# A gated-linear-attention and gated-SSM kernel: whole-row loads of w_in, the transfers of the first two xT on GpSimd's queue, and the second group's attention ahead of the first projection

## The chip, the core and the metric

The kernel runs on one core of one Trainium2 chip. The time is device microseconds of that core, from launch to end. The kernel before was timed 9 times, and one further execution was recorded by the hardware profiler.

## The reference

Two blocks follow one another. The first is a gated linear attention over 4 batches, 8 heads, 768 steps and head width 48; the second projects its output, runs a decaying sum along the sequence, gates it and projects it back.

```python
for t in range(S):                       # attention, per batch and head
    state = alpha[t, :, None] * state + k[t][:, None] * v[t][None, :]
    y[t] = q[t] @ state
x = y.transpose(0, 2, 1, 3).reshape(B, S, H * D)          # 4 x 768 x 384
proj = x @ w_in                                           # 384 x 1024
val, gate = proj[..., :512], proj[..., 512:]
for t in range(S):
    h = exp(A_log) * h + val[:, t]
    ys[:, t] = h
out = (gate * sigmoid(gate) * ys) @ w_out                 # 512 x 384
```

The two weight matrices arrive as float64. The kernel reads them as pairs of 32-bit words and makes float32 of them.

## The kernel before, in words

The sequence of each batch is cut into three groups of 256 steps, so there are 12 groups, and each group has two chunks (c = 0, 1) of 128 steps. The function `fast` does all the work; `general` is a second version that runs only if a flag that `fast` computes says that the inputs were out of its range. `fast` is scheduled by hand: every engine executes its instructions in the order in which the code issues them, and the framework adds only the waits. SP, ScalarE (ACT) and, in principle, GpSimd (POOL) can issue DMAs; each DMA reports its end through one of a few shared completion counters, and a DMA that is given a counter waits until the DMA that had it earlier has landed.

**Loads.** Groups 0 to 2 load alpha, k and q in natural layout (`pair`, `load_natural`, L411 to L421: one DMA of 196.6 KB for each chunk). Groups 3 and up load them in another layout (`loads`, `load_raw`, L396). `load_v` brings v. `load_w` (L442) brings w_in in three units of columns (128, 128 and 256 of each half), eight DMAs each, and w_out in two; the rows of w_in are reordered on the way, so that a 128-partition tile holds rows for partitions 0 to 47, 48 to 63, 64 to 111 and 112 to 127.

**Weights to float32.** `convert` (L506) makes one unit: ScalarE copies the low words (L518), VectorE (DVE) does two operations on the high words (L519, L521), and GpSimd adds both (L523). `check_w` (L525) takes the largest and smallest magnitude of each unit, late in the kernel.

**Attention of a group m.** `natural_alpha` (L558) transposes alpha on TensorE (PE), ScalarE copies it (L564). `products` (L593) makes running products of alpha with two scans on VectorE (`prod` L606 and, backwards, `inv` L618). `natural_qk` (L566) transposes k and q, and its `times` (L580) multiplies them by the products into Z. `scores` (L645) multiplies Z's k and q halves into PSUM, `masks` (L655) puts the masked result in A: half on ScalarE and GpSimd (L658, L659), half on VectorE (L660). `keys` (L636) transposes Z's keys, ScalarE copies them (L643). `state` (L686) accumulates the running state in PSUM and ScalarE copies it (S_sb, L695). `values` (L662) multiplies A by v into y, `carried` (L674) adds the part of earlier chunks. `join` (L697) copies y to xT, one half on ScalarE (L701) and one on VectorE (L702), and issues six DMAs of 16 KB that move rows of xT to other partitions (L705).

**Second block of a group n.** For each of four column blocks cc, `project` (L711) does six matmuls into pv and pg (L720), and `gated` (L724) does a scan on VectorE (hh, L727), a Silu on ScalarE (sg, L732) and a product on GpSimd (f, L733). `output` (L735) does the second projection (L741), copies and stores it. I call the work of the loop over n (L821) for one n a turn.

**Order.** Ahead of the loop stand the attention of group 0, part of that of group 1, and `convert(0)`. Turn n holds the second block of group n and, between its four projections, the attention of group n + 1 and the preparation (`products`) of group n + 2. Turn 0 also holds the rest of the conversions of w_in (`convert(1)`, `convert(2)`, `convert(2, 1)`, L850 to L872) and both of w_out (L893, L895), and turns 0 and 1 do Z's multiplications in their middle (L848, L853). In turns 0 and 1 and ahead of the loop, all six DMAs of `join` are issued by ScalarE; from turn 2 on, three by SP and three by ScalarE (L886).

## Time and profile before

| | us |
|---|---|
| median of 9 runs (lowest to highest) | 339.62 (338.27 to 342.66) |
| the profiled execution's own time | 341.38 |
| its span, first to last instruction | 339.6 |
| busy: PE, DVE, POOL, ACT | 296.4, 232.4, 105.6, 91.6 |
| mean granted TensorE clock | 0.949 |

A time in the trace counts from the start of the span. A row of a timeline gives start, duration (both us), engine, line, operation, what it writes and reads, how many were merged, and in brackets the idle time of the engine ahead of it with what ended it. An engine with a q behind it (SPq, ACTq) is its sequencer, here issuing a DMA. Lines are those of the kernel before. A busy engine may be waiting inside an instruction, so busy time alone does not show which engine sets the pace.

### The profile page before, as it was taken

Reading aid. Unit: us, or ns where it says so; the run is one execution under the profiler, and the core shown is the slowest. Engines: PE = TensorE matmul, PEld = TensorE weight load, DVE = VectorE, ACT = ScalarE, POOL = GpSimd, SP = SyncE. Lnnn points to the kernel's source line nnn. Section 1 sums busy time; section 2 is a strip of 40 time slices with the busy share of each in tenths; the row PEclk is TensorE's granted clock in tenths of the full one; section 3 lists DMA queues with packets and bytes.
Section 4 is the critical chain, followed back from the end, with each engine's and each line's share of the span. In section 5 each row is a group of like instructions: output and inputs, shape, how many; then the busy total and the mean of one; then the engine's idle time right before and its main releaser. Section 6 shows DMA issues by size and latency. Waiting matters only on the chain.

```text
span 339.6 us, 5950 instructions
## 1 busy us (share of the span) xinstructions
PE 296.4 (87%) x2341; PEld 234.4 (69%) x2341; DVE 232.4 (68%) x256; ACT 91.6 (27%) x188; POOL 105.6 (31%) x97
## 2 busy tenths in 40 slices
PE   3983869149997995999999999999999999999992
PEld 3672748127874882886887877878878788787771
DVE  3855772461994794499799899998988969633110
ACT  4161321311411411322412415124133152131111
POOL 6022272140431420080351601804416036041020
PEclk9998789878998999699999999999999999999997
DMA  9994996833208908960873937909749230100101
GB/s 135 177 175 95 174 271 127 209 46 95 67 0 188 241 12 164 245 99 12 221 144 104 225 52 188 179 12 242 123 121 223 38 93 3 58 1 14 47 5 53
DMA packets 68269, 39.71 MB, mean 117 GB/s; under 512 B 47364, under 2 KB 66952, under 8 KB 68232
## 3 DMA queue, kind: packets, MB, share of 16 engines
q1 hardware_dynamic: 65744, 38.30, 55.9%
q10 hardware_dynamic: 2488, 0.94, 1.3%
q8 instruction: 20, 0.33, 0.5%
q14 instruction: 17, 0.14, 0.1%
HBM read 33.33 MB, written 4.72 MB: 112 GB/s over the span
## 4 chain that ended last, share of the span: by engine, by line
PE 64%; DMA 12%; DVE 9%; SPq 5%; issue 4%; POOL 1%; ACTq 1%; ACT 1%; DVEq 0%; POOLq 0%
PE pv L720 17%; PE o L741 16%; PE pg L720 15%; PE sc L652 5%; DMA wbits<-in_moe_w_in_dram 5%; PE y L671 5%; DMA raw_q<-in_q_dram 3%; PE y L682 2%; PE st L692 2%; DMA raw_k<-in_k_dram 2%; SPq L420 2%; PE tp L642 2%; DVE prod L606 2%; DMA v<-in_v_dram 1%; DVE Z L597 1%
## 5 line engine op out<-in xcount | busy, mean ns | idle before, releaser
L733 POOL TENSOR_TENSOR f<-sg,hh 128x256 f32<-128x256 f32 x48 | 57.8, 1205 | 173.1 <-ACT sg L732 162.2
L720 PE MATMUL pv<-xT,w_in 128*128 128x256 f32 x288 | 77.4, 408 | 14.1 <-POOL w_in L523 9.9
L741 PE MATMUL o<-w_out,f 128*128 128x384 f32 x192 | 68.4, 510 | 14.0 <-POOL w_out L523 11.5
L720 PEld LDWEIGHTS pv<-xT,w_in 128*128 128x128 f32 x288 | 55.6, 200 | 28.1 <-POOL w_in L523 10.8
L720 PE MATMUL pg<-xT,w_in 128*128 128x256 f32 x288 | 73.2, 392 | 0.0
L741 PEld LDWEIGHTS o<-w_out,f 128*128 128x128 f32 x192 | 37.6, 197 | 39.5 <-POOL w_out L523 12.9
L720 PEld LDWEIGHTS pg<-xT,w_in 128*128 128x128 f32 x288 | 57.1, 198 | 8.6
L732 ACT ACTIVATE sg<-pg 128x256 f32<-128x256 f32 x48 | 18.4, 384 | 133.6 <-PE pg L720 77.3
L727 DVE TENSOR_TENSOR_SCAN hh<-a_dec,hh,pv 128x256 f32<-128x256 f32 x32 | 23.5, 735 | 41.4 <-PE pv L720 39.5
L659 POOL TENSOR_TENSOR A<-A,mask 128x512 f32<-128x512 f32 x24 | 31.9, 1351 | 30.1 <-ACT A L658 30.1
L606 DVE TENSOR_TENSOR_SCAN prod<-aT,first 128x1024 f32<-128x1024 f32 x12 | 32.8, 2730 | 0.1
L618 DVE TENSOR_TENSOR_SCAN inv<-aT,last 128x1025 f32<-128x1025 f32 x12 | 31.0, 2585 | 0.4
L671 PE MATMUL y<-A,v 128*64 128x128 f32 x384 | 23.9, 274 | 1.6 <-POOL A L659 1.6
L652 PE MATMUL sc<-Z 48*128 48x128 f32 x384 | 25.1, 278 | 0.1
L652 PEld LDWEIGHTS sc<-Z 48*128 48x128 f32 x384 | 22.7, 188 | 2.8 <-issue 2.1
L745 ACT ACTIVATE o_sb<-o 128x384 f32<-128x384 f32 x24 | 11.8, 490 | 47.6 <-PE o L741 47.6
L727 DVE TENSOR_TENSOR_SCAN hh<-a_dec,pv 128x256 f32<-128x256 f32 x16 | 10.9, 680 | 19.2 <-PE pv L720 19.0
L671 PEld LDWEIGHTS y<-A,v 128*64 128x64 f32 x384 | 20.7, 137 | 2.2 <-POOL A L659 2.1
L660 DVE TENSOR_TENSOR A<-sc,mask 128x512 f32<-128x512 f32 x24 | 16.4, 689 | 7.2 <-PE sc L652 6.9
L597 DVE STREAM_TRANSPOSE aT<-raw_a 128x1024 f32<-128x1024 f32 x9 | 18.4, 2040 | 0.0
L597 DVE STREAM_TRANSPOSE Z<-raw_q 128x1024 f32<-128x1024 f32 x9 | 18.3, 2035 | 0.0
L597 DVE STREAM_TRANSPOSE Z<-raw_k 128x1024 f32<-128x1024 f32 x9 | 18.2, 2020 | 0.0
(82 smaller groups left out, 251.2 us busy)
## 6 DMA issues: line engine op xcount, KB each, us to landing
raw_k<-in_k_dram SPq DMA_DIRECT2D x24, 192.0 KB, 5.0
raw_q<-in_q_dram SPq DMA_DIRECT2D x24, 192.0 KB, 5.3
v<-in_v_dram SPq DMA_DIRECT2D x24, 192.0 KB, 4.4
out_dram<-o_sb SPq DMA_DIRECT2D x24, 192.0 KB, 1.9
raw_a<-in_alpha_dram SPq DMA_DIRECT2D x23, 192.0 KB, 3.9
raw_a<-in_alpha_dram SPq DMA_DIRECT2D x18, 176.0 KB, 3.9
raw_k<-in_k_dram SPq DMA_DIRECT2D x18, 176.0 KB, 5.1
raw_q<-in_q_dram SPq DMA_DIRECT2D x18, 176.0 KB, 4.1
```

Of the source, the lines that this page charges most:

```text
L597: nc.vector.transpose(out=to.rearrange("p h (c j) -> p h j c", j=NT), in_=raw_bufs[m % NR][name].rearrange("p h (j d) -> p h j d", d=D)[:, ...
L606: nc.vector.tensor_tensor_scan(out=prod, data0=aT[:, 0:4 * GC], data1=first.rearrange("p h n -> p (h n)"), initial=0.0, op0=ALU.mult, op1= ...
L618: nc.vector.tensor_tensor_scan(out=inv[:, ::-1], data0=aT[:, ::-1], data1=last.rearrange("p h n -> p (h n)")[:, 0:4 * GC + 1][:, ::-1], in ...
L652: nc.tensor.matmul(sc[i][:, p, :], Z[rows, p, 1, cols], Z[rows, p, 0, cols], start=True, stop=True)
L659: nc.gpsimd.tensor_mul(A[:, 1], A[:, 1], mb)
L660: nc.vector.tensor_mul(A[:, 0], sc[0], mb)
L671: nc.tensor.matmul(ys[m][i][ds(64 * s, 64), e, ds(c * C, C)], v_sb[:, c, 2 * p + i, :], A[:, i, p, :], start=(c == 0 and e == 0), stop=Fal ...
L720: nc.tensor.matmul(pj, w_in[:, kk, vg, ds(cc * C, C)], xT[:, kk, :], start=(kk == 0), stop=(kk == NK - 1))
L727: nc.vector.tensor_tensor_scan(out=hh, data0=a_dec[:, cc:cc + 1].to_broadcast([C, GC]), data1=pv, initial=prev_h[cc][:, GC - 1:GC] if g el ...
L732: nc.scalar.activation(sg, pg, AF.Silu)
L733: nc.gpsimd.tensor_mul(fs[n][:, cc, :], sg, hh)
L741: nc.tensor.matmul(os[c], fs[n][:, cc, ds(c * C, C)], w_out[:, cc, :], start=(cc == 0), stop=(cc == NI - 1))
```

## The change

- w_in is loaded in whole rows (8 KB): four DMAs in place of 24, the first two (partitions 0 to 63) on SP, the other two (64 to 127) on ScalarE's queue after `masks` of group 0. k and q of group 1 are issued ahead of all weights, w_out right after v of group 1, and alpha, k and q of group 2 after that.
- The attention of group 1 is finished ahead of the loop, and with it all four conversions of w_in. Four more warming matmuls stand in PE's order ahead of it. `masks` of group 0 goes ahead of `keys`.
- Turn 0 has no attention any more. The two conversions of w_out follow the second and the third projection, and alpha of group 2 is transposed after the second. Z of group 2 is finished at the end of turn 0, not in the middle of turn 1. Turn 1 has the order of the later turns.
- In `join`, ScalarE copies both halves of y, in every group. The six DMAs of groups 0 and 1 are issued by GpSimd, those of group 2 by SP and ScalarE as in later groups.
- The buffer for the low words has two copies in place of one, and `check_w` takes the rows of w_in in three units.

SyncE's queue (SP), the start, from the loads of v of group 0 on. In the names, raw_k_83, raw_q_82 and v_85 belong to group 1, raw_a_78, raw_k_80 and raw_q_79 to group 2 here, wbits and bits to the weights. Before:

```order
L429 DMA v_84<-in_v_dram 128x8x48 x2
L450 DMA wbits_88<-in_moe_w_in_dram 48x3x256 x4
L450 DMA wbits_88<-in_moe_w_in_dram 16x3x256 x4
L420 DMA raw_k_83<-in_k_dram 128x8x48 x2
L420 DMA raw_q_82<-in_q_dram 128x8x48 x2
L450 DMA wbits_89<-in_moe_w_in_dram 48x3x256 x4
L450 DMA wbits_89<-in_moe_w_in_dram 16x3x256 x4
L429 DMA v_85<-in_v_dram 128x8x48 x2
L450 DMA wbits_90<-in_moe_w_in_dram 48x3x512 x4
L450 DMA wbits_90<-in_moe_w_in_dram 16x3x512 x4
L420 DMA raw_a_78<-in_alpha_dram 128x8x48 x2
```

And now:

```order
L429 DMA v_84<-in_v_dram 128x8x48 x2
L420 DMA raw_k_83<-in_k_dram 128x8x48 x2
L420 DMA raw_q_82<-in_q_dram 128x8x48 x2
L443 DMA bits_in<-in_moe_w_in_dram 48x3x2048
L443 DMA bits_in<-in_moe_w_in_dram 16x3x2048
L429 DMA v_85<-in_v_dram 128x8x48 x2
L448 DMA bits_out<-in_moe_w_out_dram 128x2x768 x2
L420 DMA raw_a_78<-in_alpha_dram 128x8x48 x2
L420 DMA raw_k_80<-in_k_dram 128x8x48 x2
L420 DMA raw_q_79<-in_q_dram 128x8x48 x2
```

The k and q of group 1 stand ahead of all weights, and the 24 issues of w_in have become two here (the other two are on ScalarE's queue).

GpSimd (POOL), from `masks` of group 0 on. A_254, A_265 and A_444, A_455 are the masks of groups 0 and 1 before; A_229, A_240 and A_376, A_387 now. f is the gated product. Before:

```order
L659 TENSOR_TENSOR A_254<-A_254,mask_97 128x512
L659 TENSOR_TENSOR A_265<-A_265,mask_97 128x512
L523 TENSOR_TENSOR w_in_86<-w_in_86,wr_356 128x6x128
L733 TENSOR_TENSOR f_399<-sg_410,hh_408 128x256
L523 TENSOR_TENSOR w_in_86<-w_in_86,wr_417 128x6x128
L659 TENSOR_TENSOR A_444<-A_444,mask_97 128x512
L659 TENSOR_TENSOR A_455<-A_455,mask_97 128x512
L523 TENSOR_TENSOR w_in_86<-w_in_86,wr_462 128x6x128
L733 TENSOR_TENSOR f_399<-sg_477,hh_475 128x256
L523 TENSOR_TENSOR w_in_86<-w_in_86,wr_480 128x6x128
```

And now, with xT_324 and xT_480 the xT of groups 0 and 1:

```order
L652 TENSOR_TENSOR A_229<-A_229,mask_94 128x512
L652 TENSOR_TENSOR A_240<-A_240,mask_94 128x512
L698 DMA xT_324<-xT_324 16x256 x6
L652 TENSOR_TENSOR A_376<-A_376,mask_94 128x512
L652 TENSOR_TENSOR A_387<-A_387,mask_94 128x512
L515 TENSOR_TENSOR w_in_86<-w_in_86,wr_406 128x6x128
L515 TENSOR_TENSOR w_in_86<-w_in_86,wr_411 128x6x128
L515 TENSOR_TENSOR w_in_86<-w_in_86,wr_416 128x6x128
L515 TENSOR_TENSOR w_in_86<-w_in_86,wr_421 128x6x128
L698 DMA xT_480<-xT_480 16x256 x6
L726 TENSOR_TENSOR f_503<-sg_514,hh_512 128x256
L726 TENSOR_TENSOR f_503<-sg_527,hh_525 128x256
```

Six DMAs stand ahead of the masks of group 1, the four additions for w_in stand together behind these masks, and six more DMAs stand ahead of the first product f.

TensorE (PE), from the transposes of group 1's q to the attention of group 1. Before:

```order
L574 MATMUL tn_372<-ident_96,raw_q1_82 128x128 x4
L574 MATMUL tn_377<-ident_96,raw_q1_82 128x128 x4
L720 MATMUL pv_400<-xT_347,w_in_86 128x256 x3
L720 MATMUL pg_401<-xT_347,w_in_86 128x256 x3
L642 MATMUL tp_422<-ident_96,Z_361 128x128 x4
L642 MATMUL tp_428<-ident_96,Z_361 128x128 x4
```

And now, the attention of group 1 from its keys on, in the same place:

```order
L635 MATMUL tp_388<-ident_93,Z_333 128x128 x4
L635 MATMUL tp_394<-ident_93,Z_333 128x128 x4
L685 MATMUL st_110<-v1_85,ktm0_97 64x48 x8
L664 MATMUL y0_436<-A_376,v1_85 64x128 x4
L664 MATMUL y1_437<-A_376,v1_85 64x128 x4
L664 MATMUL y0_436<-A_387,v1_85 64x128 x4
L664 MATMUL y1_437<-A_387,v1_85 64x128 x4
L685 MATMUL st_110<-v1_85,ktm1_98 64x48 x8
```

Sixteen matmuls of `carried` follow; their end and the first projections stand so:

```order
L675 MATMUL y0_436<-Z_333,S_sb_434 48x128
L675 MATMUL y1_437<-Z_333,S_sb_434 48x128
L713 MATMUL pv_504<-xT_324,w_in_86 128x256 x3
L713 MATMUL pg_505<-xT_324,w_in_86 128x256 x3
L713 MATMUL pv_517<-xT_324,w_in_86 128x256 x3
L713 MATMUL pg_518<-xT_324,w_in_86 128x256 x3
L556 MATMUL tn_530<-ident_93,raw_a0_78 128x128 x4
L556 MATMUL tn_536<-ident_93,raw_a0_78 128x128 x4
```

The first projection (pv) followed the transposes of q directly before; now the scores, keys, states and values of group 1 are ahead of it.

The diff, cut to its core:

```diff
+    bits_in = const.tile([C, NK, 2 * DI, 2], U32, name="bits_in")
+    bits_out = const.tile([C, NI, DM, 2], U32, name="bits_out")
+
+    def load_w_in(half, engine):
+        for row, size, first, step in ((64 * half, D, 4 * half * D, D), (64 * half + D, R, (4 * half + 3) * D, R)):
+            engine.dma_start(out=bits_in[ds(row, size)].rearrange("p kk n two -> p kk (n two)"),
+                             in_=moe_w_in.bitcast(U32)[ds(first, NK * step)]
+                             .rearrange("(kk p) n -> p kk n", p=step)[0:size])
...
-        r = p1.tile([C, x, y, z], I32, tag="wr", name="wr")
+        r = p2.tile([C, x, y, z], I32, tag="wr", name="wr")
...
         nc.scalar.activation(xT[:, 1::2], y[1], AF.Copy)
-        nc.vector.tensor_copy(out=xT[:, 0::2], in_=y[0])
+        nc.scalar.activation(xT[:, 0::2], y[0], AF.Copy)
...
     load_v(0, SP)
-    load_w(0, SP)
     pair("k", 1, SP, SP)
     pair("q", 1, SP, SP)
-    load_w(1, SP)
+    load_w_in(0, SP)
     load_v(1, SP)
+    for i in range(2):
+        load_w_out(i, SP)
...
+    def warm(count):
+        t = ps_mm.tile([C, 4, C], FP32, tag="mm", name="warm")
+        for _ in range(count):
+            nc.tensor.matmul(t, ident, ident[:, None, :].to_broadcast([C, 4, C]), start=True, stop=True)
+    warm(5)
...
     for c in range(G):
+        masks(0, c)
+    load_w_in(1, ACT)
+    for c in range(G):
         keys(0, c)
-    for c in range(G):
-        masks(0, c)
...
-    join(0, (ACT, ACT))
-    convert(0)()
+    join(0, (nc.gpsimd, nc.gpsimd))
     k_times, q_times = natural_qk(1, "k"), natural_qk(1, "q")
+    warm(4)
     for _ in steps:
         pass
+    for c in range(G):
+        k_times(c)
+        q_times(c)
+    for c in range(G):
+        scores(1, c)
+    for c in range(G):
+        keys(1, c)
+    for c in range(G):
+        masks(1, c)
+    for i in range(NI):
+        convert(i)()
+    state(1, 0)
+    values(1, 0)
+    values(1, 1)
+    state(1, 1)
+    carried(1, 0)
+    carried(1, 1)
+    join(1, (nc.gpsimd, nc.gpsimd))
...
-        att = m < N
+        att = 0 < n < N - 1
...
         gated(n, 1, *pj)
+        if nat:
+            natural_alpha(n + 2)
+            check_alpha(n + 2)
+            convert(NI)()
+        else:
             go(1)
         pj = project(n, 2)
         gated(n, 2, *pj)
+        if nat:
+            convert(NI + 1)()
+        else:
             go(2)
...
-            join(m, (ACT, ACT) if n < 2 else (SP, ACT))
+            join(m, (SP, ACT))
...
         if nat:
             k_times, q_times = natural_qk(n + 2, "k"), natural_qk(n + 2, "q")
+            for c in range(G):
+                k_times(c)
+                q_times(c)
```

More of the change, by code (lines that the diff above doesn't have):

```diff
@@ L781, in fast @@
     k_times, q_times = natural_qk(0, "k"), natural_qk(0, "q")
-    load_w(2, SP)
-    pair("a", 2, SP, SP)
-    for i in range(3, NW):
-        load_w(i, SP)
-    pair("k", 2, SP, SP)
-    pair("q", 2, SP, SP)
-    warm = ps_mm.tile([C, 4, C], FP32, tag="mm", name="warm")
-    for _ in range(5):
-        nc.tensor.matmul(warm, ident, ident[:, None, :].to_broadcast([C, 4, C]), start=True, stop=True)
+    for name in "akq":
+        pair(name, 2, SP, SP)
+    def warm(count):
[3 more added lines that the diff above has]
+    warm(5)
     for _ in products(0):
@@ L845, in fast @@
         gated(n, 0, *pj)
[L846 to L855 removed]
+        if att:
             attend()
@@ L858, in fast @@
             go(1)
-        if n == 1:
-            pj = project(n, 1)
-            gated(n, 1, *pj)
-            attend()
         if att:
@@ L876, in fast @@
         gated(n, 2, *pj)
-        if not nat:
+        if nat:
+            convert(NI + 1)()
+        else:
             go(2)
```

78 lines of the change are left out of this document (19 added, 59 removed).

## The prediction

> **What bounds the kernel now.** I read the page first, then busy time by stage (the windows), then TensorE's timeline with what ended its idle time, then the waits of the SP queue.
>
> ```profile
> span 339.6 us, 5950 instructions
> GB/s 135 177 175 95 174 271 127 209 46 95 67 0 188 241 12 164 245 99 12 221 144 104 225 52 188 179 12 242 123 121 223 38 93 3 58 1 14 47 5 53
> ```
>
> The windows below are cut at the first projection of each turn. The columns are the stretch, its length, busy time of PE, PEld, DVE, ACT and POOL, the granted clock, the DMA share and GB/s.
>
> ```profile
> 32.97:82.54 49.57, 33.80 (x224) 25.35 (x225) 23.79 (x27) 12.30 (x22) 15.02 (x11) 0.80 0.76 151
> 82.54:108.33 25.79, 22.85 (x182) 17.58 (x181) 21.48 (x22) 5.87 (x12) 7.76 (x6) 0.98 0.36 89
> 108.33:135.93 27.60, 23.40 (x186) 18.54 (x184) 18.92 (x18) 7.44 (x16) 6.88 (x6) 0.93 0.70 144
> 135.93:161.36 25.43, 25.43 (x201) 20.39 (x202) 19.68 (x20) 6.46 (x14) 8.96 (x6) 0.90 0.58 118
> 161.36:183.10 21.74, 21.74 (x182) 17.41 (x181) 19.74 (x21) 6.13 (x13) 8.80 (x6) 1.00 0.63 146
> 183.10:205.80 22.70, 22.70 (x188) 18.40 (x188) 20.49 (x20) 7.44 (x16) 6.90 (x6) 1.00 0.66 140
> 205.80:228.54 22.74, 22.28 (x199) 17.91 (x198) 21.76 (x22) 6.57 (x14) 8.85 (x6) 1.00 0.64 140
> 228.54:339.60 111.06, 104.14 (x811) 82.93 (x809) 66.75 (x80) 28.26 (x61) 32.94 (x28) 0.98 0.34 78
> ```
>
> From turn 4 on (161.36), PE is busy without a gap at full clock: a turn takes 21.74 to 22.74 us, and only less work for PE could shorten it. Turn 0 takes 49.57 us with 33.80 busy at clock 0.80, and turns 1 to 3 take 25.4 to 27.6. So the first 161 us hold the idle time. These rows say what PE waited for.
>
> ```profile
> 32.97 2.93 PE L720 MATMUL pv<-xT,w_in 128*128 128x256 f32 x6 [5.65 <-POOL w_in L523]
> 35.69 2.77 PE L720 MATMUL pg<-xT,w_in 128*128 128x256 f32 x6
> ...
> 48.69 2.64 PE L720 MATMUL pv<-xT,w_in 128*128 128x256 f32 x6 [2.95 <-POOL w_in L523]
> ...
> 69.59 2.93 PE L741 MATMUL o<-w_out,f 128*128 128x384 f32 x4 [8.86 <-POOL w_out L523]
> ...
> 106.31 2.23 PE L741 MATMUL o<-w_out,f 128*128 128x384 f32 x4 [2.50 <-POOL f L733]
> ...
> 135.93 0.76 PE L720 MATMUL pv<-xT,w_in 128*128 128x256 f32 x1 [4.20 <-issue]
> ```
>
> Up to 70 us PE waits for converted weights; at 106 and 136 for f and, as no engine is named, I take it, for an xT that lands late. Behind both stand SP's waits and one of its issues:
>
> ```profile
> SPq L405 <- DMA xT<-xT: 33.0, 12, 15.2
> ...
> SPq L450 <- DMA xT<-xT: 5.4, 1, 5.4
> ```
>
> ```profile
> 86.97 17.04 SPq L405 DMA_DIRECT2D raw_k<-in_k_dram  x4
> ```
>
> Loads of k and w_in share no data with xT, yet SP stood until xT transfers had landed, once for 15.2 us: four issues of raw_k took 17.04 us.
>
> **The change, part by part.** I follow the new order to the first projection (T0), then add turns.
>
> *Start to Z of group 1.* Up to group 0's scores only loads move. The rows of before that matter:
>
> ```profile
> 11.08 4.65 PE L791 MATMUL warm<-ident 128*128 128x512 f32 x10
> ...
> 26.23 1.09 PE L574 MATMUL tn<-ident,raw_q 128*128 128x128 f32 x8 [0.25 <-DVE xT L702]
> ```
>
> ```profile
> 25.51 0.66 DVE L702 COPY xT<-y 128x512 f32<-128x512 f32 x1
> 26.09 0.55 DVE L519 TENSOR_SCALAR w_in<-wbits 128x768 uint32<-128x768 uint32 x1
> 26.67 0.96 DVE L521 SCALAR_TENSOR_TENSOR w_in<-wbits,w_in 128x768 uint32<-128x768 uint32 x1
> ...
> 27.96 2.29 DVE L618 TENSOR_TENSOR_SCAN inv<-aT,last 128x1025 f32<-128x1025 f32 x1
> ...
> 36.54 0.67 DVE L580 TENSOR_TENSOR Z<-tn,inv 128x512 f32<-128x512 f32 x1
> ```
>
> The copy and the two converting operations (0.66 + 0.55 + 0.96 = 2.2 us) leave DVE's path ahead of inv, which ends at about 28.1 in place of 30.25. Four products for Z (0.6 apart) end at 30.5. On PE, q of group 1 ends at 27.3, and four warming matmuls follow: five took 4.65, so four take 3.7, to 31.0. They cover the wait for Z and cost at most 0.5 us.
>
> *Attention of group 1.*
>
> ```profile
> 39.48 2.06 PE L652 MATMUL sc<-Z 48*128 48x128 f32 x32
> ```
>
> ```profile
> 39.58 1.08 ACT L643 ACTIVATE ktm<-tp 128x512 f32<-128x512 f32 x2
> ```
>
> Scores take 31.0 to 33.0, keys to 34.0; DVE's two masks end at 33.7; on ACT two ktm and two copies of A (about 1.1 each pair) take 33.5 to 35.9, so GpSimd's first mask can start at 35.3.
>
> *The four conversions.* GpSimd's add and DVE's operations collide, and the trace shows how:
>
> ```profile
> 46.83 1.80 POOL L523 TENSOR_TENSOR w_in<-w_in,wr 128x768 int32<-128x768 int32 x1 [1.56 <-DVE w_in L521]
> ```
>
> ```profile
> 47.20 1.85 DVE L519 TENSOR_SCALAR w_in<-wbits 128x768 uint32<-128x768 uint32 x1
> ```
>
> ```profile
> 20.60 2.50 POOL L659 TENSOR_TENSOR A<-A,mask 128x512 f32<-128x512 f32 x2 [14.66 <-ACT A L658]
> ```
>
> L519 takes 0.55 us alone; started at 47.20 inside the add, it ended at 49.05, 0.42 after the add. So I let the two take turns. From 33.7 DVE does unit 0 and half of unit 1 (0.55 + 0.96 + 0.55 = 2.06, to 35.8); then in turn two masks (1.25 each), two adds (1.80 each) and, between them, 0.96 + 0.55 + 0.96 on DVE: the second add ends at 44.4. Without collisions it would be at 35.3 + 2.5 + 3.6 = 41.4.
>
> ACT now matters, for its copy of the fourth unit's low words waits for the second add's buffer, and S_sb, which the rest of the attention needs, stands behind it in ACT's order.
>
> ```profile
> 38.77 0.92 ACT L518 ACTIVATE wr<-wbits 128x768 int32<-128x768 uint32 x1
> ```
>
> ```profile
> 23.07 0.33 ACT L695 ACTIVATE S_sb<-st 128x192 f32<-128x192 f32 x1
> ```
>
> ```profile
> 53.16 0.67 PE L692 MATMUL st<-v,ktm 128*64 128x48 f32 x16
> ...
> 55.97 1.09 PE L682 MATMUL y<-Z,S_sb 48*48 48x128 f32 x32
> ```
>
> 44.4 + 0.92 + 0.33 + 0.67 + 1.09 gives T0 = 47.4, rounded to 47; without collisions 44.4. The third add ends at about 46.7 and the fourth at 49.5, ahead of their projections.
>
> *Whole rows.* For this w_in must have landed by 33.7. By then 14 loads of 196.6 KB (2.75 MB) and w_in (3.15 MB) must come, with v and w_out beside its end. The second slice of the GB/s row (177) and the sixth (271, mostly longer rows) bound the rate; a slice is 8.49 us. The first two slices (135 and 177) carry 2.65 MB, so the 14 loads are through at about 18; ACT issues its half of w_in after its two copies of A, at about 19. Counted from 20, 3.15 MB take 11.6 us at 271 (to 31.6) or 17.8 at 177 (to 37.8). I take the upper rate, as the rows get longer, not shorter; the lower one costs 4 us.
>
> *Turn 0.* PE idles about 5 us ahead of T0, so it starts slow, as at 32.97, where pv and pg took 2.93 and 2.77. Warm matmuls of a projection, transposes and the output are these:
>
> ```profile
> 84.00 1.29 PE pg L720 x6
> ```
>
> ```profile
> 80.80 1.04 PE L574 MATMUL tn<-ident,raw_k 128*128 128x128 f32 x8
> ...
> 126.40 5.32 PE L741 MATMUL o<-w_out,f 128*128 128x384 f32 x16
> ```
>
> Eight times 1.29 is 10.3, three sets of transposes 2.6 (two fill 80.80 to the first pv at 82.54), output 5.3, slow start 2.7 (about twice 2.85 less 1.46): 20.9 us, to 67.9. The scans for group 2 (2 x 2.29) and both w_out conversions fall beside it.
>
> *xT on GpSimd.* The trace has no DMA issued there. The nearest rows:
>
> ```profile
> 25.04 0.60 ACT L701 ACTIVATE xT<-y 128x512 f32<-128x512 f32 x1 [0.30 <-PE y L682]
> ...
> 57.88 4.00 ACTq L705 DMA_DIRECT2D xT<-xT  x6
> ```
>
> Six issues took ACT 4.00, or 0.67 each; as an upper bound I take 0.67 + 2.29 = 3.0, one scan of DVE ahead of each. For the first join, GpSimd has from 26.2 to 35.3, so 1.5 each is free. For the second, it starts at 49.5, and two f, an add and a third f (4.0 us) must follow before output at 61.2 needs them: 1.3 each is free. I take 1.0, near the ACT row: cost nothing. At 3.0 it costs 9 + 10 = 19 us. This takes 4 us of issuing off ACT in each early join.
>
> *Copies on ACT.* The second copy costs ACT 0.60 a turn and frees 0.67 of DVE. A copy on DVE may stand behind a scan, one on ACT need not; xT comes sooner or at worst 0.6 later, which projection 3 and the output cover (2.6 + 5.3). Nothing.
>
> *Turns 1 to 3.* With all of attention 1 and Z of group 2 done earlier, turn 1 has the form of the turn at 161.36, turn 2 of that at 183.10, turn 3 of that at 205.80: 21.74 + 22.70 + 22.74 = 67.2, against 25.79 + 27.60 + 25.43 = 78.8 now.
>
> *The rest.* 21.74 + 22.70 + 22.74 + 111.06 = 178.2, unchanged; `check_w` reads as many words as before.
>
> Sum: 47 + 20.9 + 67.2 + 178.2 = 313.3, against a span of 339.6, so 26.3 less. The profiled execution took 341.38, 0.5% above the median 339.62. I put the difference at the median: 339.62 - 26.3 = 313.3, say 313. About 0.5% is what a measurement of this kernel can tell from no change.
>
> **The rivals.**
>
> *Turns 1 to 3 keep their waits.* If SP still stands behind transfers of xT, the 11.6 us stay: 325. For it: 33.0 us of such waits. Against: GpSimd's DMAs need not share SP's counters. Chance 0.17.
>
> *Weights late.* w_in at 177 GB/s, 4 us, with v and w_out in between up to 8: 317 to 321. Against: slice six. Chance 0.1.
>
> *GpSimd is slow at issuing.* At 2 us each, the first six cost 3.0 and the second 4.2: 320. At 3.0, 332. For it: the collisions above; against: ahead of the first projection DVE does only some 6 us in the time of each join. [...] Chance 0.1.
>
> *Slower.* The same place, with a larger price: the twelve issues stand between GpSimd's masks, adds and f, which PE needs. Free are 9 + 8 = 17 us; to use up 26.3 they must take 43 together, 3.6 each, and beyond 3.7 the kernel is slower by 0.5%; at 4.0 it is 344. Against: this is six times the ACT row. Chance 0.03.
>
> *No whole-row gain and waits as before* together (w_in 8, turns 11.6, GpSimd 7): 339, no change. Chance 0.03.
>
> **How the numbers follow.** The forecast has 0.57. Its own range is 308 (no collisions, no slow start) to 318. Up to the first rival, the range reaches 326 and leaves out GpSimd's worse prices and some of what is below. Faster by over 0.5%: all but the last two, 0.94, less 0.01 for what I did not think of: 0.93; same 0.03; slower 0.04.
>
> **What would show it.** Right: the first pv at 44 to 49 with w_in landed by 34; no gap of PE over 1 us in turns 1 to 3, at 67 us for the three; SP's waits for xT short; GpSimd's issues near 1 us. Wrong: a first pv past 52, PE waiting for f in turn 0, turns of over 24 us, or weights that land after 37.

## The result, and the profile after

The changed kernel takes 325.15 us (median of 10 runs, 322.64 to 326.76) where the kernel before took 340.43 beside it: a ratio of 0.9551, with a 95% interval of 0.9519 to 0.9582. Ratios here leave out executions more than 1.5% above the fastest of the same kernel; the medians include them. The gain is 15 us where 26 were forecast. The profiled execution has a span of 325.4 against the sum's 313.3, so the miss to explain is 12.1 us.

The page's first line and its row of bytes moved (40 slices of 8.14 us; the line numbers of this section and of the experiments are those of each run's own kernel):

```profile
span 325.4 us, 5980 instructions
GB/s 134 163 155 161 126 256 176 227 73 49 233 98 87 238 75 141 221 28 170 207 44 241 112 86 237 74 150 218 23 197 182 63 48 11 52 1 14 48 5 55
```

The windows, cut as before at the first projection of each turn (length, busy time of PE, PEld, DVE, ACT and POOL, granted clock, DMA share, GB/s):

```profile
0.00:55.24 55.24, 32.99 (x323) 25.27 (x324) 31.13 (x41) 17.05 (x30) 19.27 (x32) 0.86 1.15 166
55.24:80.89 25.65, 22.77 (x92) 17.12 (x89) 14.06 (x16) 7.36 (x14) 13.97 (x13) 0.84 0.63 119
80.89:102.62 21.73, 21.73 (x183) 17.39 (x182) 19.38 (x20) 6.10 (x13) 8.81 (x6) 1.00 0.67 136
102.62:124.79 22.17, 22.17 (x186) 17.95 (x184) 18.29 (x17) 7.45 (x17) 6.91 (x6) 1.00 0.69 143
124.79:147.40 22.61, 22.61 (x202) 18.39 (x200) 19.04 (x19) 7.45 (x17) 8.98 (x6) 1.00 0.66 140
147.40:325.40 178.00, 170.80 (x1375) 136.83 (x1373) 125.22 (x133) 51.72 (x112) 57.74 (x46) 0.99 0.46 102
```

Set against the sum, row by row: T0 is 55.24 for 47 (8.2 too late), turn 0 is 25.65 for 20.9 (4.75 too long), turns 1 to 3 are 66.5 for 67.2, the rest 178.0 for 178.2. Both misses lie ahead of 81 us, and PE has no gap in turns 1 to 3. The timeline around T0, with the idle time before each row and what ended it:

```profile
18.94 24.53 SPq L448 DMA_DIRECT2D bits_out<-in_moe_w_out_dram  x2
...
44.79 0.56 DVE L511 TENSOR_SCALAR w_in<-bits_in 128x768 uint32<-128x768 uint32 x1 [12.47 <-DMA bits_in<-in_moe_w_in_dram]
45.13 1.09 PE L685 MATMUL st<-v,ktm 128*64 128x48 f32 x16 [10.86 <-DMA v<-in_v_dram]
...
51.47 0.93 ACT L510 ACTIVATE wr<-bits_in 128x768 int32<-128x768 uint32 x1 [2.03 <-POOL w_in L515]
...
52.67 0.76 PE L685 MATMUL st<-v,ktm 128*64 128x48 f32 x16 [3.00 <-ACT S_sb L688]
...
55.24 2.93 PE L713 MATMUL pv<-xT,w_in 128*128 128x256 f32 x6
```

DVE had stood for 12.47 us when w_in came, at 44.8 in place of the 31.6 that the sum used; v, queued behind w_in, came as late. The two halves of w_in, on two queues, did not move side by side. ScalarE issued its half at 18.22, but from 20 to 24 us SP's queue (q1) alone moves, and from 36 to 40 ScalarE's (q10) moves most of the bytes, at 125 and 120 GB/s:

```profile
18.22 0.82 ACTq L443 DMA_DIRECT2D bits_in<-in_moe_w_in_dram  x2
```

```profile
q1 hardware_dynamic: 61, 0.50, 97.8%
```

```profile
q10 hardware_dynamic: 78, 0.48, 94.0%
```

The columns of the last two are packets, MB and the share of the 16 DMA engines' time. From w_in's landing on, the chain is the one forecast: adds and DVE take turns (L513, 0.96 us ahead of the first add, takes 2.44 to 2.46 beside the first three), ACT's copy waits for the second add, S_sb for ACT. Then, in turn 0:

```profile
69.19 2.64 DVE L599 TENSOR_TENSOR_SCAN prod<-aT,first 128x1024 f32<-128x1024 f32 x1
69.65 3.78 POOL L515 TENSOR_TENSOR w_out<-w_out,wr 128x768 int32<-128x768 int32 x1
...
73.48 5.83 PE L734 MATMUL o<-w_out,f 128*128 128x384 f32 x12 [2.87 <-POOL w_out L515]
```

The second addition for w_out starts inside DVE's scan and takes 3.78 us where one in the first projections' chain took 1.81 to 2.00; PE waits for it 2.87 us, and then runs the twelve matmuls slowly, at a granted clock of 0.84 in this turn and of 0.52 from 73.48 to 76.40. e4 comes back to both. SP's loads of a, k and q no longer wait for transfers of xT (33.0 us before); the row is gone from the waits of SP's queue.

### The profile page after: what moved, and what is told of

It reads as the page before. It is cut to its first block, busy times and chain, and to the rows that moved or that the text cites. A ratio compares the mean times of both kernels' runs of the same rounds, so it can differ in the third digit from the quotient of the medians.

```text
span 325.4 us, 5980 instructions
## 1 busy us (share of the span) xinstructions
PE 293.1 (90%) x2349; PEld 233.0 (72%) x2349; DVE 227.1 (70%) x244; ACT 97.1 (30%) x200; POOL 115.7 (36%) x109
## 4 chain that ended last, share of the span: by engine, by line
PE 80%; DMA 9%; DVE 3%; POOL 3%; ACT 2%; issue 0%; ACTq 0%; DVEq 0%; POOLq 0%
PE pv L713 21%; PE o L734 19%; PE pg L713 19%; DMA bits_in<-in_moe_w_in_dram 8%; PE sc L645 7%; PE y L664 5%; PE y L675 3%; PE st L685 3%; PE tp L635 2%; DMA a_log<-in_moe_A_log_dram 1%; POOL w_in L515 1%; POOL w_out L515 1%; ACT wr L510 1%; DVE inv L611 1%; DVE prod L599 1%; DVE Z L573 1%
## 5 line engine op out<-in xcount | busy, mean ns | idle before, releaser
L726 POOL TENSOR_TENSOR f<-sg,hh 128x256 f32<-128x256 f32 x48 | 60.6, 1262 | 144.7 <-ACT sg L725 143.5
L713 PE MATMUL pv<-xT,w_in 128*128 128x256 f32 x288 | 73.5, 392 | 0.0
L713 PE MATMUL pg<-xT,w_in 128*128 128x256 f32 x288 | 71.0, 383 | 0.0
L734 PE MATMUL o<-w_out,f 128*128 128x384 f32 x192 | 66.0, 498 | 2.9 <-POOL w_out L515 2.9
L713 PEld LDWEIGHTS pv<-xT,w_in 128*128 128x128 f32 x288 | 53.6, 193 | 12.1 <-issue 2.2
L720 DVE TENSOR_TENSOR_SCAN hh<-a_dec,hh,pv 128x256 f32<-128x256 f32 x32 | 23.5, 733 | 33.5 <-PE pv L713 31.6
L652 POOL TENSOR_TENSOR A<-A,mask 128x512 f32<-128x512 f32 x24 | 30.0, 1271 | 35.6 <-ACT A L651 35.6
L611 DVE TENSOR_TENSOR_SCAN inv<-aT,last 128x1025 f32<-128x1025 f32 x12 | 29.4, 2449 | 0.4
L685 PE MATMUL st<-v,ktm 128*64 128x48 f32 x320 | 13.5, 229 | 13.9 <-DMA v<-in_v_dram 10.9
L685 PEld LDWEIGHTS st<-v,ktm 128*64 128x64 f32 x320 | 11.8, 142 | 17.8 <-issue 14.0
L664 PEld LDWEIGHTS y<-A,v 128*64 128x64 f32 x384 | 22.4, 145 | 0.2 <-issue 0.2
```

The costliest lines, as they stand in the source:

```text
L611: nc.vector.tensor_tensor_scan(out=inv[:, ::-1], data0=aT[:, ::-1], data1=last.rearrange("p h n -> p (h n)")[:, 0:4 * GC + 1][:, ::-1], in ...
L652: nc.gpsimd.tensor_mul(A[:, 1], A[:, 1], mb)
L664: nc.tensor.matmul(ys[m][i][ds(64 * s, 64), e, ds(c * C, C)], v_sb[:, c, 2 * p + i, :], A[:, i, p, :], start=(c == 0 and e == 0), stop=Fal ...
L685: nc.tensor.matmul(st[ds(64 * i, 64), p, :], ktms[c][:, p, i, :], vs[m % NV][:, c, 2 * p + i, 0:D], start=(ch == 0 and p == 0), stop=(ch = ...
L713: nc.tensor.matmul(pj, w_in[:, kk, vg, ds(cc * C, C)], xT[:, kk, :], start=(kk == 0), stop=(kk == NK - 1))
L720: nc.vector.tensor_tensor_scan(out=hh, data0=a_dec[:, cc:cc + 1].to_broadcast([C, GC]), data1=pv, initial=prev_h[cc][:, GC - 1:GC] if g el ...
```

## The experiments

The times of all twelve, with T0 and the lengths of turns 0, 1 and 2 from the windows of each profiled execution (us); ratios are to the kernel before, run on the same chip:

| kernel | time | ratio, 95% interval | T0 | turn 0 | turn 1 | turn 2 |
|---|---|---|---|---|---|---|
| before | 340.43 | | 33.0 | 49.6 | 25.8 | 27.6 |
| changed | 325.15 | 0.9551 (0.9519 to 0.9582) | 55.2 | 25.7 | 21.7 | 22.2 |
| e1 w_in over 128 partitions | 317.56 | 0.9337 (0.9274 to 0.9401) | 45.9 | 25.6 | 21.7 | 22.2 |
| e2 w_in in 24 pieces | 324.11 | 0.9540 (0.9474 to 0.9605) | 48.1 | 25.0 | 25.1 | 22.2 |
| e3 attention first | 320.14 | 0.9403 (0.9333 to 0.9472) | 47.7 | 26.8 | 21.7 | 22.2 |
| e4 w_out together | 320.91 | 0.9430 (0.936 to 0.95) | 54.7 | 20.7 | 21.7 | 22.2 |
| e5 xT on ScalarE | 336.69 | 0.9887 (0.9848 to 0.9925) | 68.2 | 22.5 | 21.7 | 22.2 |
| e6 copy on VectorE | 325.35 | 0.9516 (0.9457 to 0.9575) | 55.3 | 24.7 | 21.7 | 22.2 |
| e7 halves in turn | 322.52 | 0.9481 (0.9418 to 0.9545) | 49.3 | 22.7 | 25.3 | 22.2 |
| e8 combined | 319.26 | 0.9364 (0.9318 to 0.941) | 45.2 | 22.6 | 25.4 | 23.9 |
| e9 pieces, third xT on GpSimd | 321.55 | 0.9388 (0.9317 to 0.946) | 48.4 | 24.8 | 21.7 | 25.6 |
| e10 before, xT on GpSimd | 340.35 | 0.9982 (0.9951 to 1.0013) | 38.8 | 47.6 | 23.9 | 26.8 |
| e12 combined, third xT on GpSimd | 318.95 | 0.9333 (0.9286 to 0.9381) | 46.7 | 22.5 | 21.7 | 25.3 |
| e13 w_in by 64 partitions | 319.30 | 0.9344 (0.927 to 0.9418) | 46.5 | 22.6 | 21.7 | 22.2 |

### e1: the same rows, all partitions at once

```diff
-        for row, size, first, step in ((64 * half, D, 4 * half * D, D), (64 * half + D, R, (4 * half + 3) * D, R)):
-            engine.dma_start(out=bits_in[ds(row, size)]..., in_=moe_w_in...)
+        for kk in range(2 * half, 2 + half):
+            engine.dma_start(out=bits_in[:, kk].rearrange("p n two -> p (n two)"),
+                             in_=moe_w_in.bitcast(U32)[ds(kk * C, C)])
```

> The changed kernel with w_in loaded in whole rows of 8 KB, but each third of its rows into all 128 partitions (two transfers on SP, one on ScalarE's queue) in place of 48, 16, 48 and 16 partitions. Left out: the reordering of the rows, so the products are those of other rows. Destination theory (the rate is set by how few partitions a transfer writes): w_in lands by 30 us in place of 44.8, the 8 KB rows take under 500 ns each in place of 800 to 1000, the first projection starts at 46 to 48 in place of 55.2, about 317 us. Row theory (8 KB rows are slow wherever they go) and queue theory (ScalarE's half waits until SP's is through): w_in lands at 42 or later, 324 to 326 us.

What the DMA view says of the changed kernel between 19 and 27 us, when nearly all packets are those of w_in, into 48 partitions of the lower half:

```profile
DMA packets 136, 1.06 MB, mean 132 GB/s; under 512 B 7, under 2 KB 7, under 8 KB 7
```

And of e1 between 20 and 24 us:

```profile
DMA packets 221, 1.68 MB, mean 420 GB/s; under 512 B 16, under 2 KB 16, under 8 KB 16
```

The length of the rows, 8 KB, and the bytes are the same; only the destination differs, and the rate is 3.2 times as high. DVE starts on w_in when the rest of its work is done, without a wait, and T0 follows 13.8 us later:

```profile
32.13 0.55 DVE L510 TENSOR_SCALAR w_in<-bits_in 128x768 uint32<-128x768 uint32 x1
```

T0 is 45.90, just below the 46 to 48 of the destination theory. The sum had said 47 for weights that are there by 33.7, so its working of the chain holds, and the load is what failed. Within the chain two terms miss in opposite directions: the second add ends at 41.8 for 44.4, as ACT's copy behind it shows, and from there to T0 it is 4.1 us for 3.0.

```profile
41.81 0.91 ACT L509 ACTIVATE wr<-bits_in 128x768 int32<-128x768 uint32 x1 [1.57 <-POOL w_in L514]
```

Turn 0 stays at 25.59: it has a cause of its own.

### e2: the 24 pieces of before

```diff
-    load_w_in(1, ACT)
...
+        for col, w in ((0, C), (C, C), (2 * C, 2 * C)):
+            for rows in (((0, D, 0, D), (64, D, 4 * D, D)), ((D, R, 3 * D, R), (64 + D, R, 7 * D, R))):
+                for vg in range(2):
+                    for row, size, first, step in rows:
+                        engine.dma_start(out=bits_in[ds(row, size), :, ds(vg * DI + col, w)]..., in_=...)
```

> The changed kernel with the whole-row part undone: w_in comes in the 24 pieces of before (rows of 1 and 2 KB, alternating between partitions 0 to 63 and 64 to 127), all on SP, in the place of the first whole-row transfer. Row theory and destination theory with alternating halves: at the 177 GB/s of before's second slice, 3.15 MB take 18 us, w_in lands at 36 to 38, the first projection starts at 48 to 50, 318 to 320 us. Queue theory, and the theory that w_in's rate does not depend on the pieces: lands at 44 to 46, 325 us. If whole rows are a gain after all: later than 46, over 327 us.

Conversion starts at 37.27 in place of 44.79 and T0 is 48.05, so the short pieces, with the two halves in turn, arrive 7.5 us sooner than the whole rows. The median moves by 1 us only: its five executions spread from 318.96 to 324.78, and turn 1 grew by 3.4 us:

```profile
73.05:98.18 25.13, 21.90 (x183) 17.25 (x181) 19.39 (x20) 6.63 (x14) 8.82 (x6) 1.00 0.57 120
```

The waits of SP's queue in that turn (us in total, times, longest) have the row of before again:

```profile
SPq L405 <- DMA xT<-xT: 12.0, 2, 11.7
```

In this stage the order is that of the changed kernel; only the number of transfers ahead of it differs. e8 to e12 come back to this.

### e3: the second group's attention ahead of w_in

```diff
-    load_w_in(0, SP)
     load_v(1, SP)
+    load_w_in(0, SP)
...
-    for i in range(NI):
-        convert(i)()
     state(1, 0)
...
     join(1, (nc.gpsimd, nc.gpsimd))
+    for i in range(NI):
+        convert(i)()
```

> The changed kernel with v of group 1 loaded ahead of w_in, and state, values, carried and join of group 1 issued ahead of the four conversions. Theory that the copies of the low words on ScalarE and the late v hold up the first projection beyond w_in's landing: it starts after the first GpSimd addition, about 3.7 us after w_in lands; w_in lands 0 to 2.4 us later than 44.8, so the first projection at 48.5 to 51, 319 to 321 us. Rival, that the projections then wait for each of the four additions in turn: first projection early, but the fourth block of turn 0 no earlier than now, 324 to 325 us.

```profile
47.69 2.93 PE L713 MATMUL pv<-xT,w_in 128*128 128x256 f32 x6 [8.76 <-POOL w_in L515]
```

T0 falls to 47.69, 0.8 below the lower end expected, and now waits for the weights alone; conversion still starts only at 43.95. Of the 7.5 us that T0 gains, 1.1 come back in turn 0 (26.78), which now starts with the conversions still running.

### e4: both w_out conversions after the second projection

```diff
             convert(NI)()
+            convert(NI + 1)()
...
-        if nat:
-            convert(NI + 1)()
-        else:
+        if not nat:
             go(2)
```

> The changed kernel with both conversions of w_out after the second projection of turn 0, so that the second addition on GpSimd no longer meets VectorE's scan of group 2. Theory that this collision made the output of turn 0 wait 2.87 us and then run at half clock: turn 0 falls from 25.65 to 21 to 22 us, 320.5 to 322 us. Rival, that the waiting addition only moves on to f or to the third projection: 324 to 326 us.

```profile
54.66:75.32 20.66, 20.21 (x92) 15.78 (x89) 13.85 (x15) 7.20 (x14) 13.08 (x13) 0.92 0.74 147
```

Moved ahead of the scan, the addition is done in time, PE's wait of 2.87 goes to 0.45, the clock in the turn is 0.92 in place of 0.84, and turn 0 is 20.66: the forecast was 20.9. The turn is 5.0 us shorter, and the wait accounts for 2.4 of them. The rest is the speed of PE, and this does not hang on the collision alone. In e5, e7 and e13 below, the order of the w_out conversions is that of the changed kernel and PE waits the same 2.86 us for the same addition, but the twelve matmuls then take 4.14 us, not 5.83, at a clock of 0.95 to 0.96 for the turn, which is 22.5 to 22.7 us long. In e7:

```profile
66.30 4.14 PE L734 MATMUL o<-w_out,f 128*128 128x384 f32 x12 [2.86 <-POOL w_out L515]
```

So the collision is shown for about half of turn 0's miss. The other half goes with the granted clock, and why that is low in some of these executions is not shown.

### e5: xT on ScalarE again

```diff
-    join(0, (nc.gpsimd, nc.gpsimd))
+    join(0, (ACT, ACT))
...
-    join(1, (nc.gpsimd, nc.gpsimd))
+    join(1, (ACT, ACT))
```

> The changed kernel with one part undone: the twelve transfers of xT of groups 0 and 1 are issued by ScalarE again. Theory (counters): SyncE's and ScalarE's transfers share eight completion counters, so that a load on SyncE that reuses the counter of a transfer of xT cannot be issued before that transfer is; with xT back on ScalarE, SyncE's loads ahead of the first projection (group 3) and in turn 0 are held until xT of group 1 goes out at about 57, SyncE shows some 10 to 30 us of waits for xT more than the changed kernel's 51, and one of turns 1 to 3 shows a gap of TensorE of over 1 us; ScalarE issues six in 4.0 us where GpSimd took 3.0, and the S_sb copies behind come later. Time 327 to 333. Rival (order alone): the new order of the second group's attention had already taken the waits out of turns 1 to 3, and the queue of xT makes no difference: 324 to 326, turns 1 to 3 still 66.5. Rival (GpSimd): the six issues on GpSimd, 3 us, stand ahead of f and the w_out additions, and ScalarE has room: 322 to 324.

The time is 11.5 us above the changed kernel's, more than any theory gave, and none of it is in turns 1 to 3: these are 21.70, 22.20 and 22.60 in the windows. It is all ahead of T0, which comes 12.9 us later (turn 0 is 3.1 shorter, at the higher clock). ScalarE's timeline:

```profile
24.50 0.59 ACT L695 ACTIVATE xT<-y 128x512 f32<-128x512 f32 x1
44.67 11.65 ACTq L698 DMA_DIRECT2D xT<-xT  x6
56.36 1.08 ACT L636 ACTIVATE ktm<-tp 128x512 f32<-128x512 f32 x2 [31.27 <-DMA xT<-xT]
```

xT of group 0 was ready at 25.1, but its first transfer was issued at 44.67 and the six took until 56.3, and ktm of group 1 stood behind them in ScalarE's order for 31.27 us. Each transfer names a completion counter in the trace: SP and ACT take theirs from the same eight (100 and 102 to 108), GpSimd from others (111 to 118). The six on ScalarE reuse counters of v, w_out and the loads of a, k and q of group 2, which SP had queued behind w_in, and an issue waits for the counter's former user. So the queue matters by 11.5 us here, but as a blockade of ScalarE by the weights, not of SP by xT.

### e6: the copy of y[0] on VectorE again

```diff
-        nc.scalar.activation(xT[:, 0::2], y[0], AF.Copy)
+        nc.vector.tensor_copy(out=xT[:, 0::2], in_=y[0])
```

> The changed kernel with one part undone: the copy of y[0] to xT is VectorE's again, 8 to 9 copies of about 0.6 us. Theory: in the steady turns TensorE sets the pace and the copy is beside it on either engine; in the chain ahead of turn 0 it is one of two copies that ScalarE does after one another (0.6 us each), and VectorE is held by GpSimd's operations there, so it comes out even: 324.5 to 326, turns 1 to 3 within 0.3 of 66.5. Rival: VectorE is late in the turns (19.4 of 21.7 us busy), and 0.6 us more on it makes TensorE wait for hh: 327 to 331, all turns longer by about 0.5. Rival: two engines share the copies, xT is ready 0.6 earlier at the first projection: 324 to 324.6.

```profile
80.00:101.70 21.70, 21.70 (x183) 17.32 (x182) 20.52 (x21) 5.50 (x12) 7.07 (x6) 1.00 0.62 134
```

DVE is 1.1 us busier than in the changed kernel's turn 1 (20.52 for 19.38) and the turn is as long. The time, 325.35, can't be told from 325.15: this part of the change is worth nothing, as forecast.

### e7: whole rows, the two halves in turn

```diff
+        for kk in range(NK):
+            for row, first, step in ((0, 0, D), (64, 4 * D, D), (D, 3 * D, R), (64 + D, 7 * D, R)):
+                engine.dma_start(out=bits_in[ds(row, step), kk].rearrange("p n two -> p (n two)"),
+                                 in_=moe_w_in.bitcast(U32)[ds(first + kk * step, step)])
...
-    load_w_in(1, ACT)
```

> The changed kernel with w_in in whole rows of 8 KB, in the right order, in twelve transfers on SyncE's queue: for each of the three row blocks, partitions 0 to 47, 64 to 111, 48 to 63, 112 to 127, in turn. Theory (destination): packets of 8 KB are slow (0.8 to 1.1 us) while one half of the partitions alone is written, and 0.31 us where all 128 are; short transfers of the two halves that follow each other overlap over the 16 engines, so w_in lands at 33 to 38, the first pv starts at 46 to 50 and the time is 316 to 321. If an engine ends its share of one transfer long before the next begins, so that halves don't overlap, w_in lands at 42 to 46 as in the changed kernel and the time is 323 to 326. Rival (few long transfers against many short ones, whatever the destination): the same as the version in 24 pieces, w_in at 36, first pv 48, 319 to 324. What may spoil the total: the number of transfers shifts which loads share a counter with a transfer of xT, which can put one wait of 3 to 5 us into turns 1 to 3.

From 20 to 28 us, and at the start of turn 2:

```profile
DMA packets 243, 1.37 MB, mean 171 GB/s; under 512 B 77, under 2 KB 77, under 8 KB 77
```

```profile
97.27 1.53 PE L713 MATMUL pv<-xT,w_in 128*128 128x256 f32 x6 [3.37 <-DMA xT<-xT]
```

Better than 132, far from 420: by this rate, transfers to the two halves one after the other mostly did not overlap here. Conversion starts at 39.26, just past the 33 to 38 of the first theory, and T0 is 49.3, inside its range; the total, 322.52, is above its 321, with the wait that the expectation named, here 3.37 us. The experiment doesn't tell its theory from its rival, which gave nearly the same numbers; e13 does.

### e8: three edits together

e7's load, e3's order and e4's conversions in one kernel.

> Three edits together: w_in in whole rows with the halves in turn, v of the second group and that group's attention ahead of w_in and its conversions, both w_out conversions after the second projection. Theory: the first pv waits only for w_in's conversions, which start when the rows land (33 to 38) and take TensorE to about 4 us after the first: first pv at 40 to 45; turn 0 is 20.7 to 22 and the rest as measured, 244.5 to the end: 306 to 312. Rival: turn 0's gates queue on VectorE behind the other conversions, so that what the first pv gains comes back as a longer turn 0: 312 to 317. Rival: halves in turn don't help: w_in at 44, first pv 47.7, turn 0 22: 314 to 316.

T0 is 45.2 and turn 0 22.6, each a little past the upper end of the first theory (45 and 22). But turn 1 is 25.4 and turn 2 23.9, which no theory had, and the time is 319.26 where the highest of them ended at 317. SP and, last, ScalarE and TensorE around turn 1:

```profile
69.16 3.42 SPq L405 DMA_DIRECT2D raw_k<-in_k_dram  x4
84.81 2.11 SPq L405 DMA_DIRECT2D raw_q<-in_q_dram  x4
86.98 1.05 SPq L429 DMA_DIRECT2D v<-in_v_dram  x2
88.34 2.92 SPq L698 DMA_DIRECT2D xT<-xT  x3
```

```profile
82.93 1.87 ACTq L698 DMA_DIRECT2D xT<-xT  x3
```

```profile
93.16 2.90 PE L713 MATMUL pv<-xT,w_in 128*128 128x256 f32 x6 [3.49 <-DMA xT<-xT]
```

Here is the whole chain of such a turn. ScalarE's three transfers of xT have the counters 100, 102 and 104, and three of the four loads of q the same three. SP's first load of q reuses the counter of the one that ScalarE issues at 82.93, so SP stands from 72.6 to 84.8; behind q and v stands SP's own half of the same xT, which goes out at 88.34 and is late for the projection at 93.16.

### e9 and e12: the third xT on GpSimd as well

To e2 (e9) and to e8 (e12):

```diff
-            join(m, (SP, ACT))
+            join(m, (nc.gpsimd, nc.gpsimd) if n < 2 else (SP, ACT))
```

> The version in 24 pieces with one more edit: xT of groups 1 and 2 of the loop, so of groups 0 to 2 in all, goes out on GpSimd's queue, where the third had SyncE and ScalarE. Theory (counters): the 3.2 us gap of TensorE in that version's turn 1 comes from four loads of q that reuse the completion counters of ScalarE's three transfers of xT and so could not be issued for 11.7 us; with xT on GpSimd's own counters SyncE has no such wait in turn 1, turn 1 falls from 25.1 to 21.7 to 22 and the time by about 3.3, to 316 to 318 in the profiled span. Rival (the transfers of xT are late because of traffic or ScalarE's work, and the counter only records it): turn 1 stays at 25 and the span at 320 to 321.

> The combined version (halves of w_in in turn, second group's attention ahead of w_in's conversions, w_out's conversions together) with xT of the third group on GpSimd's queue as well. Theory (counters): the 3.5 us that the first pv of turn 2 waited for xT go, turn 1 falls from 25.4 to 21.7 to 22, span 314 to 315, time 315 to 316.5. Rival (the wait is traffic): no change, 319.

In both, turn 1 falls to 21.7 as the counters theory said, and in both the wait is back one turn later. e12's SP, ACT and PE in turn 2:

```profile
95.39 3.26 SPq L405 DMA_DIRECT2D raw_k<-in_k_dram  x4
108.38 2.01 SPq L405 DMA_DIRECT2D raw_q<-in_q_dram  x4
```

```profile
106.52 1.87 ACTq L698 DMA_DIRECT2D xT<-xT  x3
```

```profile
116.19 1.53 PE L713 MATMUL pv<-xT,w_in 128*128 128x256 f32 x6 [2.93 <-DMA xT<-xT]
```

It follows the first xT that ScalarE issues in a turn. So the cause is the counter and not the traffic, but moving one transfer only moves the wait. The totals were expected to fall by 3. e12 against e8 is 0.9333 against 0.9364, with overlapping intervals; e9's median is 2.6 below e2's, but its four executions spread from 319.38 to 324.51, and in the profiled ones its turn 4 starts 1.6 us later than e2's. e12 has the lowest median of the versions that keep w_in's rows in the order of the heads, 318.95, below the changed kernel as well as below the kernel before; e8 can't be told from it.

### e10: the kernel before with GpSimd's queue alone

```diff
-    join(0, (ACT, ACT))
+    join(0, (nc.gpsimd, nc.gpsimd))
...
-            join(m, (ACT, ACT) if n < 2 else (SP, ACT))
+            join(m, (nc.gpsimd, nc.gpsimd) if n < 2 else (SP, ACT))
```

> The kernel before with one part of the change alone: xT of groups 0 to 2 on GpSimd's queue. Theory (counters set turns 1 to 3): SyncE's waits for xT ahead of loads of a, k and q fall from 33.0 us to under 10, the issue of raw_k that took 17 us takes 2, and turns 1 to 3, 78.8 us, become 67 to 72; time 328 to 334, ratio 0.965 to 0.98. Rival (the order sets turns 1 to 3): they stay at 77 to 79, since the attention of the second group and Z of the third stand in turn 1 whatever the queue; SyncE's waits may go, the time stays within 2 us of before. Rival (GpSimd): its 18 issues of 0.5 us stand ahead of the additions for which TensorE waits in turn 0 (8.9 us for w_out), and turn 0 grows by 2 to 6 us.

```profile
88.09 1.79 SPq L405 DMA_DIRECT2D raw_k<-in_k_dram  x4
...
115.29 2.19 SPq L405 DMA_DIRECT2D raw_k<-in_k_dram  x4
129.09 2.00 SPq L405 DMA_DIRECT2D raw_q<-in_q_dram  x4
```

The issue of raw_k that took 17.04 us takes 1.79, and turn 1 is 23.9 for 25.8. In turn 2 SP stands behind ScalarE's part of the next xT just as before, and turns 1 to 3 are 75.0 in place of 78.8: a third of the 11.6 us, and between the 67 to 72 of the theory and the 77 to 79 of the rival. Even that is lost again ahead of turn 0:

```profile
38.83 2.90 PE L720 MATMUL pv<-xT,w_in 128*128 128x256 f32 x6 [11.37 <-DMA xT<-xT]
```

GpSimd had issued the first xT by 30; it landed 9.5 us after its issue (the DMA view's median between 20 and 40 us), where ScalarE's landed after 1.9 in the kernel before. The sum is no change, 0.9982.

### e13: half of the partitions, evenly

```diff
+        engine.dma_start(out=bits_in[ds(64 * half, 64)].rearrange("p kk n two -> p kk (n two)"),
+                         in_=moe_w_in.bitcast(U32).rearrange("(kk p) n -> p kk n", p=C)[ds(64 * half, 64)])
```

> The changed kernel with w_in in plain row order, so without the reordering by heads, in two transfers of 64 partitions by three rows of 8 KB: partitions 0 to 63 on SyncE, 64 to 127 on ScalarE. It tells apart why the transfers of 48 and 16 partitions were slow (0.8 to 1.3 us a packet). [...] Rival (the uneven count of 48 and 16 is the whole cause): packets take 0.31, w_in lands at 30 to 33, first pv 46, time 317 to 318 as over 128 partitions. Rival (half the partitions cost the same whatever the count): 0.8 to 1.1, lands at 42 to 45, time 324 to 326.

From 19 to 24 us, while SP's transfer to partitions 0 to 63 moves, and the first conversion:

```profile
DMA packets 125, 1.02 MB, mean 205 GB/s; under 512 B 0, under 2 KB 0, under 8 KB 0
```

```profile
35.41 1.49 DVE L509 TENSOR_SCALAR w_in<-bits_in 128x768 uint32<-128x768 uint32 x1 [2.91 <-DMA bits_in<-in_moe_w_in_dram]
```

Half of the partitions got 205 GB/s, half of 420, and 48 of them got 132, less than 48/64 of 205 (154). So one half of the partitions alone is what cost most, and the uneven 48 and 16 cost some more. Here too the halves followed one another: no packet of ScalarE's queue moves in these 5 us, though its half was issued at 18.46. From 125 packets in 5 us, with the 16 DMA engines busy for 98.8% of them, I estimate 0.63 us a packet; e1's 420 GB/s with rows of 8 KB makes 0.31. Neither rival of the expectation fits, the one with 0.31 or the one with 0.8 to 1.1, and the landing, 35.4 at the latest, lies between their 30 to 33 and 42 to 45. The four times lie between 314.79 and 506.62 us, so the total says nothing here. Why one half alone is slow was not shown. T0, 46.5, is only 0.6 us later than in e1: with w_in there by 35, a faster load was worth little to T0.

## Why the prediction was right, and 12 us short

The forecast was 313. That 325.15 still lies inside its range is luck: the range reached 326 for the first rival, whose 11.6 us of waits in turns 1 to 3 did not come, and the 12 us that did come have other places. Two of its signs of being wrong were there, a first pv past 52 (55.2) and weights that land after 37.

**T0, the step that failed: "I take the upper rate, as the rows get longer, not shorter; the lower one costs 4 us".** The bounds, 177 and 271 GB/s, came from slices in which transfers to both halves of the partitions were under way, and the trace of before already spoke against row length. The faster part of the sixth slice is w_out, whose transfers write all 128 partitions; w_in's own 2 KB pieces, twice as long as those of the second slice, moved no faster than that slice. Before, from 35 to 42 us (w_in) and from 46 to 49 (w_out):

```profile
DMA packets 693, 1.22 MB, mean 174 GB/s; under 512 B 97, under 2 KB 97, under 8 KB 693
```

```profile
DMA packets 401, 1.19 MB, mean 397 GB/s; under 512 B 15, under 2 KB 15, under 8 KB 400
```

The changed load writes partitions 0 to 47 alone for some 9 us (1152 KB at the 132 GB/s measured), and the other ranges mostly after them, since ScalarE's half did not move beside SP's (no packet of q10 from 20 to 24 us). A row's length was the wrong variable: the pieces of 1 and 2 KB (e2) beat rows of 8 KB by 7.5 us. w_in landed 13 us late, of which 8.2 reached T0. The rival "weights late" had this place with 4 to 8 us.

**T0 given the weights: right.** e1 measured 45.90 for 47, with DVE and GpSimd taking turns as worked out (DVE's L510 there, 0.55 us alone, took 1.62 and 2.15); inside the chain a miss of 2.6 us one way and one of 1.1 the other partly cancel.

**Turn 0: "both w_out conversions fall beside it" failed.** That DVE and GpSimd collide (before, L519 took 0.55 us alone and 1.85 inside the add) was applied to the four conversions of w_in, not to the two of w_out; the second met the scan, and PE waited 2.87 us. That is about half of the 4.75; the other half is PE's slower running at a clock of 0.84, which three runs with the same wait don't have (e5, e7, e13). In e4, without the collision and at 0.92, the turn is 20.66 for 20.9.

**Turns 1 to 3 and the rest: right in size (66.5 for 67.2, 178.0 for 178.2), half right in reason.** The prediction gave the gain to GpSimd's own counters and to the new order. The runs point to the order: with xT on ScalarE the turns stay free (e5), and with GpSimd alone in the old order they keep two thirds of the waits (e10). But e5 also shifts by twelve the transfers that share the eight counters, so it does not isolate the queue. That the changed kernel has no such wait in turn 1 also hangs on which transfers happen to share a counter: e2, e7 and e8, with the same order from there on and 24 or 12 transfers of w_in in place of 4, have it. Which count does and which doesn't is not settled here beyond these cases.

**xT on GpSimd: "cost nothing" right, and worth more than forecast at another place.** Six issues:

```profile
57.10 2.94 POOL L698 DMA_DIRECT2D xT<-xT  x6
```

0.49 us each, below the 1.0 taken, so the rival of slow issuing fell. The six of group 0 took 3.08 us, though VectorE's scan ran until 26.69:

```profile
25.27 3.08 POOL L698 DMA_DIRECT2D xT<-xT  x6 [4.69 <-ACT xT L695]
```

What the queue brought is that ScalarE did not stand behind counters held by weights: 11.5 us by e5.

**The copies on ScalarE: nothing, right** (e6).

The misses add up: 8.2 + 4.75 - 0.7 - 0.2 = 12.05 of 12.1. The first has a tested cause, the second has one for about half of it; no single version was run with all partitions and w_out together, so that such a one would reach 313 is argued from e1 and e4 only.

## What to carry to other kernels

Here a load's rate was set by which partitions were being written at the time, more than by the length of its rows (8 KB rows at 420 GB/s into 128, 132 into 48): put all 128 under one transfer where the layout allows it, and don't carry a rate over from a stage with another destination. Where operations of two engines delay each other (here an addition for w_out beside a scan, 3.78 us for 1.81 to 2.00), look for every pair in the new order, not only in the place that was rearranged. And before a transfer is put on a queue, ask whose completion counter it will reuse: here an issue waited for a transfer that it shared nothing with (raw_k for xT, up to 15.2 us before), and the engine instruction queued behind such an issue waited too (ktm, 31.27 us in e5).

## What the runs showed of the hardware that was not expected

- Rows of 8 KB from DRAM moved at 420 GB/s into 128 partitions (e1), 205 into 64 of one half (e13), 132 into 48 of one half (the changed kernel).
- Transfers to the two halves mostly moved one after the other, whether they followed on one queue (171 GB/s, e7) or stood on two (132 GB/s from 19 to 27 us in the changed kernel, 205 from 19 to 24 in e13, and no packet of ScalarE's queue in the latter).
- GpSimd issued a transfer of sixteen rows of 1 KB in 0.49 to 0.51 us, less than ScalarE's 0.67 in the kernel before; but behind the weights it landed late. The DMA view of the changed kernel between 20 and 45 us, and that of e12 between 80 and 92 (KB each, median us to landing):

```profile
xT<-xT POOLq DMA_DIRECT2D x6, 16.0 KB, 15.9
```

```profile
xT<-xT POOLq DMA_DIRECT2D x6, 16.0 KB, 1.6
```

  Hidden in the changed kernel, this cost 5.9 us of T0 in e10.
- The two issues of w_out took SP 24.53 us from 18.94 on, until w_in was nearly through; why these took that long was not tested. Everything that SP would issue next came later by that.
